# Attention stage: the k rows and the result rows are split into two 16-bit parts first and turned by transposing DMAs instead of on TensorE

## The chip, the cores and the metric

The kernel runs on one core of one Trainium2 chip. A core has five engines, each with an instruction queue that it works off in order: TensorE (PE; its weight loads are listed apart as PEld), VectorE (DVE), ScalarE (ACT), GpSimd (POOL) and SyncE (SP), which here only issues DMAs. The metric is the device time of one execution in microseconds; lower is better. Times are medians of runs, and one further execution was profiled.

## The reference, cut to what matters

```python
def _attn_ref(q, k, v, alpha):                # B, H, S, D = 4, 8, 768, 48
    state = np.zeros((B, H, D, D)); y = np.zeros_like(q)
    for t in range(S):
        state = alpha[:, :, t, :, None] * state + np.einsum('bhd,bhe->bhde', k[:, :, t], v[:, :, t])
        y[:, :, t] = np.einsum('bhd,bhde->bhe', q[:, :, t], state)
    return y

def reference(...):
    attn_out = _attn_ref(q, k, v, alpha)
    x = attn_out.transpose(0, 2, 1, 3).reshape(B * S, H * D)     # 3072 tokens x 384
    x = _moe_ref(x, ...)       # 8 experts, all of them on all tokens, Sinkhorn weights
    return _moe2_ref(x, ...)   # 8 experts, the best two of each token
```

## The kernel before, in words

The program runs three stages one after the other: the gated linear attention, a dense mixture of experts, and a sparse one. Matrix products that need more than 16 bits are made of two 16-bit parts of each operand (a high part, and what is left over), in three products.

The change touches the attention. It works in chunks of 128 tokens: 6 chunks of each of 4 batches, 24 chunks in all, numbered i (chunk c = i // 4 of batch i % 4). A table written out by hand, `order_of`, says in which order the pieces of different chunks are recorded; in each turn i, from the fifth on, that is p1 of chunk i, the four loads of chunk i+3, p3 of chunk i-2, p2 and p2b of chunk i-1, p4 of chunk i-2 and p5 of chunk i-3:

- **p1** (VectorE): two scans over alpha (`ce`, line 420, backwards; `bh`, line 424), the scaled keys `ks` (line 422) and queries `qs` (line 425); GpSimd makes `g`, the old state times the decay of the chunk, in two instructions (line 431, chunks from the fifth on); ScalarE and VectorE split v into `vh`.
- **p2**: TensorE transposes the four 128x128 blocks of `ks` (line 444) and ScalarE and VectorE split the result into the two parts of `ktok` (lines 446, 447). TensorE multiplies `ks` and `qs` into scores (line 454), ScalarE copies them out into the buffer `AFB` (which lies in the tile `acc`, line 456, two instructions), and GpSimd masks them in place (line 457, two instructions). There is one such buffer for all chunks.
- **p2b**: ScalarE and VectorE split the masked scores into the two parts of `am` (lines 464, 465).
- **p3**: TensorE multiplies `g` with `qs` (line 473), `am` with `vh` (line 478) and, in the first 20 chunks, `ktok` with `vh` (line 485); VectorE adds the latter to the state (line 489 or 491), ScalarE copies the result `y` out (line 493).
- **p4**: TensorE transposes the three blocks of `y` (line 502), ScalarE and VectorE split them into `xh` and `xl` (lines 504, 505).
- **p5**: router products of the first mixture (lines 513, 514), put into `lg` by VectorE (line 518).

Between these pieces a loop puts matmuls of the first expert (the stream: line 212, evacuated on lines 216 and 217; line 225, evacuated on line 237), a fixed amount of them for each piece, as soon as p4 of the chunk that they need has been recorded. The order on every engine is therefore fixed when the program is built. The weights of that expert are loaded and split (lines 144, 146) during the first turns.

The names of the profile: `acc` is also `AFB`, `wt` also holds loaded q and v, `bank` is a bank of PSUM, `la` and `lk` are loaded alpha and k.

Of the kernel before, what the change touches and what calls it, by code (L numbers as in the profile page):

```python
# [46 lines left out]
def kernel(ctx, tc, q, k, v, alpha, w_gate, w1a, w2a, g2w, n2w, noise, w1b, w2b, out):  # L47
# [34 lines left out]

    xh = pp.tile([128, KC, N], F16, name="xh")
    xl = pp.tile([128, KC, N], F16, name="xl")
    acc = pp.tile([128, NT, DM], F32, name="acc")
# [281 lines left out]


    INV = ap_.tile([128, NP, C2], F32, name="inv")
    nc.vector.memset(INV, 0.0)  # L370
    nc.vector.memset(INV[:, :, C2 - 1:], 1.0)

# [40 lines left out]
    def p1(i):  # L413
        c, b = order[i]
        qt, kt, at = LQ[i % NL], LK[i % NL], LA[i % NL]
        ce = CE[i % 2]
        bh = ar.tile([128, NP, C2], F32, name="bh", bufs=1)
        qs = ar.tile([128, NP, C], F32, name="qs", bufs=3)
        ks = ar.tile([128, NP, C], F32, name="ks")
        nc.vector.tensor_tensor_scan(flat(ce)[:, ::-1], flat(at)[:, ::-1], flat(INV)[:, ::-1], initial=0.0,  # L420
                                     op0=OP.mult, op1=OP.add)
        nc.vector.tensor_mul(ks, kt, ce[:, :, 2:])
        nc.vector.reciprocal(INV[:, :, 0], ce[:, :, 1])
        nc.vector.tensor_tensor_scan(flat(bh), flat(at), flat(INV), initial=0.0, op0=OP.mult, op1=OP.add)
        nc.vector.tensor_mul(qs, qt, bh[:, :, 1:C + 1])
        G = None
        if c:
            g = GB[i % 3]
            for s in range(2):
                h = slice(64 * s, 64 * s + 64)  # L430
                nc.gpsimd.tensor_mul(g[h, :, s, :], ST[b][h, :, s * D:(s + 1) * D],
                                     ce[h, :, 1:2].to_broadcast([64, NP, D]))
            G = g.rearrange("p r a d -> p r (a d)")
        vh = ar.tile([128, 2, H, D], F16, name="vh", bufs=3)
        vt = LV[i % NV]
        nc.scalar.activation(vh[:, 0], vt, AF.Copy, scale=SK)
        nc.vector.scalar_tensor_tensor(vh[:, 1], vt, SK, vh[:, 0], op0=OP.mult, op1=OP.subtract)
        R[i] = [qs, ks, G, vh]

    def p2(i):  # L440
        qs, ks, G, vh = R[i]
        pt = bank([128, NP, C])
        for r in range(NP):
            nc.tensor.transpose(pt[:, r, :], ks[:, r, :], ident)
        kt = ar.tile([128, 2, NP, C], F16, name="ktok")
        nc.scalar.activation(kt[:, 0], pt, AF.Copy, scale=SK)
        nc.vector.scalar_tensor_tensor(kt[:, 1], pt, SK, kt[:, 0], op0=OP.mult, op1=OP.subtract)
        pA = [bank([128, NP, C]), bank([128, NP, C])]
# [6 lines left out]
        for s in range(2):  # L455
            nc.scalar.activation(af[:, s], pA[s], AF.Copy, scale=SK)
            nc.gpsimd.affine_select(af[:, s], af[:, s], pattern=[[0, NP], [1, 128]], compare_op=OP.is_ge, fill=0.0,
                                    base=0, channel_multiplier=-1)
        R[i] += [kt, am]

# [6 lines left out]
    def p3(i):  # L467
# [13 lines left out]
        if c + 1 < NC:  # L481
# [6 lines left out]
            if c:  # L488
                nc.vector.tensor_add(ST[b], pv, G)
            else:  # L490
                nc.vector.tensor_copy(ST[b], pv)
        y = ar.tile([128, DM], F32, name="y")
        nc.scalar.activation(y, py.rearrange("p r a d -> p (r a d)"), AF.Copy, scale=SX / (SK * SK))
        R[i].append(y)

    def p4(i):
        c, b = order[i]
        T = c * B + b
        y = R[i][-1]
        px = bank([128, KC, 128])  # L500
        for kc in range(KC):
            nc.tensor.transpose(px[:, kc, :], y[:, kc * 128:(kc + 1) * 128], ident)
        s = slice(T * 128, (T + 1) * 128)
        nc.scalar.activation(xh[:, :, s], px, AF.Copy)
        nc.vector.tensor_sub(xl[:, :, s], px, xh[:, :, s])

# [802 lines left out]
```

## Time and profile before

| | us |
|---|---|
| median of 3 runs (lowest, highest) | 2095.74 (2094.11, 2097.69) |
| the profiled execution | 2102.97 |
| its span, first to last instruction | 2101.2 |
| what lies around the span | 1.8 |
| TensorE busy | 2016.1 (96%) |
| VectorE busy | 1229.3 (59%) |
| ScalarE busy | 725.8 (35%) |
| GpSimd busy | 625.4 (30%) |

The shares are means over stages with different limits. The attention with its part of the stream takes up about the first 247 of the 2101 us; what follows is recorded without any use of the lines above. Within the attention the unit to read is one turn, the time from one line's instruction for chunk i to the same line's for chunk i+1.

### The profile page before, as it was taken

The numbers are of one execution on the slowest core, as the hardware profiler recorded it, in microseconds if no ns is written. First come the engines' busy times: TensorE is split into PE (matmuls) and PEld (weight loads), VectorE is DVE, ScalarE is ACT, GpSimd is POOL, SyncE is SP. The second block draws the span as 40 slices with busy tenths as digits, with TensorE's granted clock in tenths as the row PEclk, the third lists the DMA queues.
The fourth block names the chain that finished last, engine by engine and source line by source line (L and its number), as shares of the span: only waits on it lengthen the run. The fifth ranks groups of instructions, "written<-read, shape, count | busy, mean of one in ns | idle before, by whom it ended". The sixth has DMA issues, their size and how long they took to land. (4 is left out here: it accounts for less than half of the span.)

```text
span 2101.2 us, 38370 instructions
## 1 busy us (share of the span) xinstructions
PE 2016.1 (96%) x16123; PEld 1361.2 (65%) x16123; DVE 1229.3 (59%) x2513; ACT 725.8 (35%) x1277; POOL 625.4 (30%) x452
## 2 busy tenths in 40 slices
PE   6999999999999999999999999999999999999996
PEld 5887656667766766677667766775556565555553
DVE  8889574765675585566557556554345655444431
ACT  5554422432342243333333333223334233333230
POOL 2433212522442253234324332230001243323322
PEclk9999999999999999999999999999999999999998
DMA  6333010100010020010001001004112334433331
GB/s 212 96 105 105 21 41 21 47 16 1 26 36 1 1 61 2 1 34 29 1 11 51 1 1 41 1 2 152 57 42 84 84 91 121 96 73 87 84 76 23
DMA packets 61855, 106.94 MB, mean 51 GB/s; under 512 B 10980, under 2 KB 44029, under 8 KB 61680
## 3 DMA queue, kind: packets, MB, share of 16 engines
q1 hardware_dynamic: 50256, 85.05, 12.7%
q0 software_dynamic: 11136, 18.89, 5.2%
q8 instruction: 127, 2.08, 0.4%
q10 hardware_dynamic: 288, 0.52, 0.1%
q14 instruction: 48, 0.39, 0.1%
HBM read 85.17 MB, written 21.63 MB: 51 GB/s over the span
## 5 line engine op out<-in xcount | busy, mean ns | idle before, releaser
L272 PE MATMUL bank<-xh,wt 128*128 128x512 f16 x1728 | 521.9, 380 | 6.2 <-DVE ss L295 3.8
L306 PE MATMUL long<-wt,hid 128*128 128x192 f16 x6048 | 508.8, 246 | 14.1 <-DVE acc L316 9.2
L291 POOL TENSOR_TENSOR hid<-ss,hid 128x1024 f16<-128x1024 f32 x144 | 307.1, 2132 | 706.1 <-ACT hid L290 651.7
L306 PEld LDWEIGHTS <-hid 128*128 128x128 f16 x6048 | 499.6, 98 | 27.0 <-issue 11.1
L272 PEld LDWEIGHTS <-wt 128*128 128x128 f16 x2592 | 253.1, 98 | 306.2 <-PE bank L272 6.1
L225 PE MATMUL bank<-wt,hid 128*128 128x384 f16 (+1 forms) x2496 | 430.5, 328 | 1.8 <-DVE hid L866 1.8
L225 PEld LDWEIGHTS <-hid 128*128 128x128 f16 (+1 forms) x2496 | 242.2, 99 | 156.6 <-issue 5.2
L272 PE MATMUL bank<-xl,wt 128*128 128x512 f16 x864 | 328.2, 380 | 0.0
L316 DVE SCALAR_TENSOR_TENSOR acc<-long,Pm,acc 128x192 f32<-128x192 f32 (+1 forms) x360 | 187.3, 533 | 169.8 <-PE long L306 167.5
L295 DVE SCALAR_TENSOR_TENSOR ss<-bank,ss 128x256 f32<-128x256 f32 x576 | 241.5, 421 | 58.3 <-ACT hid L284 39.6
L295 DVE SCALAR_TENSOR_TENSOR hid<-bank,hid 128x256 f16<-128x256 f32 (+1 forms) x288 | 158.9, 552 | 180.9 <-ACT ss L279 180.9
L290 ACT ACTIVATE hid<-ss 128x1024 f16<-128x1024 f32 x144 | 152.2, 1057 | 241.2 <-DVE ss L295 241.2
L146 DVE SCALAR_TENSOR_TENSOR wt<-wst,wt 128x1024 f16<-128x1024 f32 (+3 forms) x129 | 167.2, 1308 | 36.9 <-ACT wt L144 36.1
L278 ACT ACTIVATE hid<-bank 128x256 f16<-128x256 f32 x144 | 53.4, 371 | 382.4 <-PE bank L272 382.4
L875 POOL DMA_INDIRECT out_dram<-acc,ix x56 | 91.5, 1634 | 296.5 <-DVE acc L874 245.6
L862 PEld LDWEIGHTS <-wt 128*128 128x128 f16 x1152 | 110.9, 98 | 86.4 <-issue 4.7
L866 DVE SCALAR_TENSOR_TENSOR hid<-bank,hid 128x384 f16<-128x384 f32 (+1 forms) x128 | 74.9, 589 | 109.5 <-ACT hid L865 109.3
L865 ACT ACTIVATE hid<-bank 128x384 f16<-128x384 f32 (+1 forms) x128 | 65.8, 517 | 205.1 <-PE bank L862 201.6
L144 ACT ACTIVATE wt<-wst 128x1024 f16<-128x1024 f32 (+3 forms) x129 | 111.4, 883 | 70.9 <-DMA wst<-in_moe_w_dram 47.3
L194 PE MATMUL bank<-xh,wt 128*128 128x512 f16 x384 | 120.0, 379 | 0.7 <-DVE acc L316 0.7
L862 PE MATMUL bank<-xh,wt 128*128 128x384 f16 (+1 forms) x576 | 109.1, 343 | 0.9 <-ACT xh L852 0.9
L284 ACT ACTIVATE hid<-bank 128x512 f16<-128x512 f32 x144 | 86.0, 597 | 66.4 <-PE bank L272 66.4
(188 smaller groups left out, 1792.7 us busy)
## 6 DMA issues: line engine op xcount, KB each, us to landing
wst<-in_moe_w_dram SPq DMA_DIRECT2D x45, 512.0 KB, 3.3
wst<-in_moe_w_dram SPq DMA_DIRECT2D x60, 384.0 KB, 3.2
la<-in_alpha_dram SPq DMA_DIRECT2D x24, 260.0 KB, 2.7
lk<-in_k_dram SPq DMA_DIRECT2D x24, 256.0 KB, 3.0
wt<-in_q_dram SPq DMA_DIRECT2D x22, 256.0 KB, 3.9
out_dram<-zero SPq DMA_DIRECT2D x6, 768.0 KB, 4.4
xd<-x SPq DMA_DIRECT2D x24, 192.0 KB, 1.9
wt<-in_v_dram SPq DMA_DIRECT2D x16, 192.0 KB, 4.1
```

The source lines that it names most:

```text
L144: nc.scalar.activation(t[:, o:o + n], src, AF.Copy, scale=SW)
L146: nc.vector.scalar_tensor_tensor(t[:, o + o1:o + o1 + n], src, SW, t[:, o:o + n], op0=OP.mult, op1=OP.subtract)
L194: nc.tensor.matmul(p, w1s(e, a, kc, f), x[:, kc, s], start=(n == 0), stop=(n == 3 * KC - 1))
L225: nc.tensor.matmul(p, h(a, f, s), w2s(x, b, f), start=(f + n == 0), stop=(f == FC - 1 and n == 2))
L272: nc.tensor.matmul(p, w1s(e, a, kc, f), x[:, kc, tok], start=(n == 0), stop=(n == 3 * KC - 1))
L290: nc.scalar.activation(lefts(e, nb, j, 0, S1, 4), sums, AF.Copy)
L291: nc.gpsimd.tensor_sub(lefts(e, nb, j, 1, S1, 4), sums, lefts(e, nb, j, 0, S1, 4))
L295: nc.vector.scalar_tensor_tensor(out, p, 0.0, x, op0=OP.max, op1=op)
L306: nc.tensor.matmul(out, left(e, nb, j, a, aop)[:, q * 128:(q + 1) * 128], w2t(e, b, wop, j), start=start and n == 0, stop=stop and n == 3 ...
L316: nc.vector.scalar_tensor_tensor(a, p, Pm[:, T, e:e + 1], a, op0=OP.mult, op1=OP.add)
L862: nc.tensor.matmul(p, w1s(x, a, kc, f), xt[:, b * KC + kc, :], start=(i == 0), stop=(i == 3 * KC - 1))
L875: nc.gpsimd.indirect_dma_start(out=out, out_offset=bass.IndirectOffsetOnAxis(ap=ix, axis=0), in_=y, in_offset=None, bounds_check=N - 1, oo ...
```

## The change

Before, `ks` and `y` (32-bit) are transposed on TensorE and split into two 16-bit parts behind that. After, they are split first and a transposing DMA turns both parts in one go.

- `ks` is scaled by 256 through the start values of the scan, so that it needs no factor in the split. In p1, for the first 20 chunks, ScalarE makes the high part `kf[:, 0]`, GpSimd the low part `kf[:, 1]`, and SP issues a DMA transpose of both (8 blocks of 128x128) into `ktok`.
- p2 loses its four transposes and both instructions of the split.
- In p3 ScalarE and VectorE split `y` on its way out of PSUM, the state's sum becomes one instruction with a factor on `g`.
- In p4 only a DMA transpose of the two parts of `y` (6 blocks of 128x128) into `x2` is left; `xh` and `xl` are the two halves of `x2`.

```diff
-    xh = pp.tile([128, KC, N], F16, name="xh")
-    xl = pp.tile([128, KC, N], F16, name="xl")
+    x2 = pp.tile([128, 2 * KC, N], F16, name="x2")
+    xh, xl = x2[:, :KC], x2[:, KC:]
...
-    nc.vector.memset(INV[:, :, C2 - 1:], 1.0)
+    nc.vector.memset(INV[:, :, C2 - 1:], SK)
...
         ks = ar.tile([128, NP, C], F32, name="ks")
+        kf = ar.tile([128, 2, NP, C], F16, name="kf")
+        kt_ = ar.tile([128, 2, NP, C], F16, name="ktok")
...
         nc.vector.tensor_mul(qs, qt, bh[:, :, 1:C + 1])
+        if c + 1 < NC:
+            nc.scalar.activation(kf[:, 0], ks, AF.Copy)
+            nc.gpsimd.tensor_sub(kf[:, 1], ks, kf[:, 0])
+            nc.sync.dma_start_transpose(out=kt_.rearrange("p a r c -> p (a r) c"),
+                                        in_=kf.rearrange("p a r c -> p (a r c)"))
         G = None
...
-        R[i] = [qs, ks, G, vh]
+        R[i] = [qs, ks, G, vh, kt_]
...
-        qs, ks, G, vh = R[i]
-        pt = bank([128, NP, C])
-        for r in range(NP):
-            nc.tensor.transpose(pt[:, r, :], ks[:, r, :], ident)
-        kt = ar.tile([128, 2, NP, C], F16, name="ktok")
-        nc.scalar.activation(kt[:, 0], pt, AF.Copy, scale=SK)
-        nc.vector.scalar_tensor_tensor(kt[:, 1], pt, SK, kt[:, 0], op0=OP.mult, op1=OP.subtract)
+        qs, ks, G, vh, kt = R[i]
...
-                nc.vector.tensor_add(ST[b], pv, G)
+                nc.vector.scalar_tensor_tensor(ST[b], G, 1.0 / SK, pv, op0=OP.mult, op1=OP.add)
...
-        y = ar.tile([128, DM], F32, name="y")
-        nc.scalar.activation(y, py.rearrange("p r a d -> p (r a d)"), AF.Copy, scale=SX / (SK * SK))
+        y = ar.tile([128, 2, DM], F16, name="y")
+        py = py.rearrange("p r a d -> p (r a d)")
+        nc.scalar.activation(y[:, 0], py, AF.Copy, scale=SX / (SK * SK))
+        nc.vector.scalar_tensor_tensor(y[:, 1], py, SX / (SK * SK), y[:, 0], op0=OP.mult, op1=OP.subtract)
...
-        px = bank([128, KC, 128])
-        for kc in range(KC):
-            nc.tensor.transpose(px[:, kc, :], y[:, kc * 128:(kc + 1) * 128], ident)
         s = slice(T * 128, (T + 1) * 128)
-        nc.scalar.activation(xh[:, :, s], px, AF.Copy)
-        nc.vector.tensor_sub(xl[:, :, s], px, xh[:, :, s])
+        nc.sync.dma_start_transpose(out=x2[:, :, s], in_=y.rearrange("p a d -> p (a d)"))
```

The order on the engines moves at three places. First GpSimd, in the middle of the attention: two turns of before,

```order
L431 TENSOR_TENSOR g_112<-acc,ce_118 64x4x48 x2
L457 AFFINE_SELECT acc<-acc 128x512 x2
L431 TENSOR_TENSOR g_113<-acc,ce_119 64x4x48 x2
L457 AFFINE_SELECT acc<-acc 128x512 x2
L431 TENSOR_TENSOR g_114<-acc,ce_118 64x4x48 x2
```

and two turns of after, where the masking is line 459 and the product with the state line 439:

```order
L431 TENSOR_TENSOR kf<-ks,kf 128x512
L439 TENSOR_TENSOR g_113<-acc,ce_117 64x4x48 x2
L459 AFFINE_SELECT acc<-acc 128x512 x2
L431 TENSOR_TENSOR kf<-ks,kf 128x512
L439 TENSOR_TENSOR g_111<-acc,ce_118 64x4x48 x2
```

The subtraction for chunk i now stands ahead of the two products of chunk i, and so ahead of the masking of chunk i-1. Second ScalarE, one turn of before, from the split of v of chunk i to the split of the scores of chunk i-1,

```order
L436 ACTIVATE vh<-wt_72 128x384
L493 ACTIVATE y<-bank 128x384
L446 ACTIVATE ktok<-bank 128x512
L456 ACTIVATE acc<-bank 128x512 x2
L464 ACTIVATE am<-acc 128x1024
```

and the same turn of after, with the next one's beginning:

```order
L430 ACTIVATE kf<-ks 128x512
L444 ACTIVATE vh<-wt_71 128x384
L496 ACTIVATE y<-bank 128x384
L458 ACTIVATE acc<-bank 128x512 x2
L466 ACTIVATE am<-acc 128x1024
L517 ACTIVATE pr<-bank 128x8
```

The high part of k is now made at the head of the turn, ahead of v, y and the scores, and `xh` (line 504 of before) is gone. Third SP, one turn of after:

```order
L505 DMA_TRANSPOSE x_66<-y 128x6x128
L432 DMA_TRANSPOSE ktok<-kf 128x8x128
L366 DMA la_82<-in_alpha_dram 128x520
L366 DMA lk_79<-in_k_dram 128x512
L366 DMA wt_71<-in_q_dram 128x512
L366 DMA wt_71<-in_v_dram 128x384
```

Before, only the four loads stood there. On VectorE the split of `ktok` (line 447) and `xl` (line 505) are gone and the low part of `y` (line 497 of after) stands right behind the state's sum; the rest stands as it did.

## Rows read from the trace of the kernel before

**Rows 1.** Busy time of each engine in two stretches of the attention (windows).

```profile
core 0: us, PE busy (x) PEld busy (x) DVE busy (x) ACT busy (x) POOL busy (x), PEclk, DMA share, GB/s
43.39:199.32 155.93, 148.05 (x1873) 124.70 (x1871) 139.59 (x214) 78.56 (x156) 60.89 (x65) 1.00 0.32 103
199.32:247.50 48.18, 45.42 (x519) 36.53 (x517) 36.41 (x56) 23.71 (x47) 16.35 (x18) 1.00 0.07 22
```

**Rows 2.** Timeline of GpSimd: start, length, line, idle before and its releaser.

```profile
43.39 2.35 POOL L431 TENSOR_TENSOR g<-acc,ce 64x192 f32<-64x192 f32 x2 [7.54 <-DVE ce L420]
...
97.80 1.22 POOL L457 TENSOR_SCALAR_AFFINE_SELECT acc<-acc 128x512 f32<-128x512 f32 x2 [2.70 <-ACT acc L456]
103.21 2.35 POOL L431 TENSOR_TENSOR g<-acc,ce 64x192 f32<-64x192 f32 x2 [4.18 <-PE bank L444]
105.64 1.88 POOL L457 TENSOR_SCALAR_AFFINE_SELECT acc<-acc 128x512 f32<-128x512 f32 x2
...
199.32 2.35 POOL L431 TENSOR_TENSOR g<-acc,ce 64x192 f32<-64x192 f32 x2 [4.60 <-DVE ce L420]
```

**Rows 3.** Timeline of VectorE, from one split of scores to the next.

```profile
100.14 1.23 DVE L465 TENSOR_TENSOR am<-acc,am 128x1024 f16<-128x1024 f32 x1 [2.50 <-ACT am L464]
101.29 0.55 DVE L505 TENSOR_TENSOR xl<-bank,xh 128x384 f16<-128x384 f32 x1
101.75 0.15 DVE L518 TENSOR_TENSOR lg<-bank,pr 128x8 f32<-128x8 f32 x1
101.83 1.23 DVE L420 TENSOR_TENSOR_SCAN ce<-la,inv 128x520 f32<-128x520 f32 x1
103.09 0.69 DVE L422 TENSOR_TENSOR ks<-lk,ce 128x512 f32<-128x512 f32 x1
...
109.20 1.21 DVE L465 TENSOR_TENSOR am<-acc,am 128x1024 f16<-128x1024 f32 x1
```

**Rows 4.** Timeline of ScalarE in the same turn.

```profile
107.55 1.06 ACT L464 ACTIVATE am<-acc 128x1024 f16<-128x1024 f32 x1 [0.63 <-POOL acc L457]
```

**Rows 5.** Groups by line and shape, 43.39 to 199.32 us: busy, mean ns, idle before.

```profile
L217 DVE SCALAR_TENSOR_TENSOR hid<-bank,hid 128x512 f16<-128x512 f32 x18 | 12.2, 677 | 0.1
L447 DVE SCALAR_TENSOR_TENSOR ktok<-bank,ktok 128x512 f16<-128x512 f32 x16 | 10.8, 674 | 0.0
L444 PE MATMUL bank<-ident,ks 128*128 128x128 f32 x64 | 9.8, 275 | 0.0
L446 ACT ACTIVATE ktok<-bank 128x512 f16<-128x512 f32 x16 | 9.5, 596 | 16.6 <-PE bank L444 16.4
L502 PE MATMUL bank<-ident,y 128*128 128x128 f32 x48 | 8.1, 278 | 0.0
```

**Rows 6.** The nearest subtraction on GpSimd, whole run (groups by line).

```profile
L291 POOL TENSOR_TENSOR hid<-ss,hid 128x1024 f16<-128x1024 f32 x144 | 307.1, 2132 | 706.1 <-ACT hid L290 651.7
```

**Rows 7.** Who waited for whom, 43.39 to 199.32 us: total, times, longest.

```profile
PE bank L478 <- DVE am L465: 7.8, 12, 1.3
```

**Rows 8.** DMA, 43.39 to 199.32 us: queue (packets, MB, share); issues (KB, us to landing).

```profile
q1 hardware_dynamic: 9216, 15.80, 31.6%
...
lk<-in_k_dram SPq DMA_DIRECT2D x16, 256.0 KB, 3.0
```

**Rows 9.** Timeline of TensorE in the first two turns with stream matmuls.

```profile
21.20 0.55 PE L502 MATMUL bank<-ident,y 128*128 128x128 f32 x3
...
25.10 0.26 PE L212 MATMUL bank<-xl,wt 128*128 128x128 f16 x1 [2.06 <-DVE xl L505]
...
34.87 0.50 PE L502 MATMUL bank<-ident,y 128*128 128x128 f32 x3
...
37.61 0.22 PE L212 MATMUL bank<-xl,wt 128*128 128x128 f16 x1 [0.92 <-DVE xl L505]
```

**Rows 10.** Timeline of TensorE behind a long wait, in the next stage.

```profile
313.35 0.38 PE L272 MATMUL bank<-xh,wt 128*128 128x512 f16 x1 [2.45 <-DVE acc L235]
...
313.78 0.59 PE L272 MATMUL bank<-xh,wt 128*128 128x512 f16 x2
...
316.79 1.06 PE L272 MATMUL bank<-xh,wt 128*128 128x512 f16 x2
```

More of the change, by code (lines that the diff above doesn't have):

```diff
@@ L458, in p2 @@
                                     base=0, channel_multiplier=-1)
-        R[i] += [kt, am]
+        R[i] += [am]
     def p2b(i):
```

## Prediction, made before the changed kernel was run

> **What bounds the kernel now.** I read the windows first, to see which engine is full in the stretch that the change touches. From the product with the state of chunk 4 to that of chunk 20 [rows 2], sixteen turns, 155.93 us pass, 9.75 us a turn. In it TensorE is busy for 148.05 us and VectorE for 139.59 us [rows 1]: 9.25 and 8.72 us a turn, so TensorE idles 0.5 us a turn and VectorE 1.0. Neither has room to spare, and neither is simply full: nearly all of TensorE's idle time, 7.8 of 7.9 us, is spent before line 478 waiting for VectorE's split of the scores [rows 7]. So I took the timelines next, to see what that split waits for. It is the end of a row of steps that hand over between engines: VectorE makes `ce` and `ks`, GpSimd multiplies the state with `ce` and then masks the scores, ScalarE splits off their high part, VectorE the low part [rows 2 to 4]. In the turn shown GpSimd's products start at 103.21, right behind `ce`, the masking ends at 107.52, ScalarE is through at 108.61, and VectorE, which had other work until then, takes up the split at 109.20. So this row of steps is now some 0.6 us shorter than VectorE's own work beside it. GpSimd itself is 39% busy (60.89 of 155.93 us), with its order fixed.
>
> **The change part by part.** *Removed.* TensorE loses four and three transposes a turn, 9.8 and 8.1 us over sixteen turns, 1.12 us a turn [rows 5]; 8.13 us of its 9.25 are left. VectorE loses line 447, 0.67 us a turn [rows 5]; the low part of `y` has the shape and source of `xl` (0.55 us [rows 3]) and replaces it one for one, and the state's sum stays one instruction. VectorE is left with 8.05 us. ScalarE swaps one copy of 512 columns for another and loses `xh`. If these two engines alone set the pace, a turn would take some 0.7 to 1.1 us less.
>
> *Moved.* The work that takes their place stands elsewhere, and this decides. The subtraction of `kf` is on GpSimd ahead of the products with the state and of the masking, and it has to wait for ScalarE's `kf`, which waits for `ks` of the same turn. Before, GpSimd began its products when `ce` was there; now it begins two engines later. This closes a ring: VectorE does not reach `ks` of the next turn until it has made the split of the scores of this one, and that split now hangs on this turn's `ks`. From the end of `ks` once round:
>
> - ScalarE's `kf`: 0.60 (line 446, 512 columns [rows 5]) and 0.03 to hand over (107.52 to 107.55 [rows 2, 4]);
> - GpSimd's subtraction: half of a line 291, which does the same on 1024 columns in 2132 ns [rows 6]: 1.07, and 0.03;
> - the two products: 2.43, from 103.21 to the start of the masking at 105.64 [rows 2];
> - the two maskings to ScalarE's start: 1.91, 105.64 to 107.55 [rows 2, 4];
> - ScalarE's split of the scores: 1.06 [rows 4]; VectorE's: 0.03 and 1.15 (100.14 to 101.29 [rows 3]);
> - `lg` 0.08, `ce` 1.26, `ks` 0.69 (101.75 to 103.78 [rows 3]).
>
> That is 10.34 us. In 5 of the 16 turns line 217 stands between the split and `lg` in VectorE's order, 0.68 us each [rows 5], 0.21 on the mean: 10.55 us a turn. VectorE's own work between the end of `ks` and the split, 5.4 us now (103.78 to 109.20) and 5.3 after (0.67 less, 0.55 more), no longer covers the 7.2 us that the other engines take. So a turn gets 0.80 us longer where it could have got shorter: 16 x 0.80 = 12.8 us. The bounds: the two maskings take 1.88 us when they follow directly on the products and 1.22 when GpSimd stood waiting before them [rows 2]; with 1.22 the ring is 9.9 and the sum +2. If the products, which now follow directly on the subtraction, cost those 0.66 us more too, it is 11.2 and +23. I take the middle value, because in the ring the maskings always follow directly on the products.
>
> What else stands behind the new waits: on ScalarE, `kf` is ahead of v, of `y`, of the stream's `hid` and of the copies of the scores. All of these slip behind `ks`, but they need only be done when GpSimd is through with the products, 3.5 us after `kf`, and add up to about 3 us; this I cost at nothing, and it is the next thing to be late if GpSimd is faster than I think.
>
> *Added on SP.* A transposing DMA of k waits for GpSimd's subtraction and, for its buffer, for line 485 two turns back; behind it in SP's queue stand the four loads for a chunk three turns ahead. A load lands in 3.0 us [rows 8] and has some 29 us, so that wait is covered. k itself is needed two turns later (21 us), `y` in the router's products most of a turn later. The DMA queue is busy 31.6% of the stretch, 3.1 us a turn for 964 KB [rows 8]; the transposes add 256 and 192 KB. The trace shows no transposing DMA. By their bytes they would take 1.4 us of the 16 engines a turn; if every 256-byte row of a block costs as much as a mean packet of now (31.6% of 155.93 us x 16 / 9216 = 0.085 us), 1792 of them take 9.6 us. They differ from a load mainly in the way they write, not in bytes, so I take a value near the first, covered by the ring's slack up to some 7 us a turn.
>
> *The start and the end.* Stream matmuls of the first two turns need the first `x` at once: from line 502 to the first use of `xl` 3.9 and 2.7 us pass now [rows 9], mostly in VectorE's queue. A DMA that lands in 3.0 us or more, issued behind five loads, replaces this, though its source is ready earlier: I take +2.5 us for both turns, from -1 to +8. In the last four turns nothing of k is left; there TensorE is busy 45.42 of 48.18 us [rows 1] and loses 4 x 1.12 us, but the last `x` comes by DMA and costs about 1.5 of that back: -3, from -4.5 to 0.
>
> *Sum.* 12.8 + 2.5 - 3 = +12.3 us on the profiled execution's 2102.97 (0.34% above the median of the runs): on the median, 2095.74 + 12.3 = **2108 us**. After the attention the order is unchanged, TensorE runs nearly without a break, and nothing can take a delay up.
>
> **The rivals.** *The ring is shorter than VectorE's work* (faster): if the four steps off VectorE take 5.3 us and not 7.2, for instance because GpSimd's recorded spans overlap more than they say, VectorE sets the pace and 24 turns gain its 0.67 us, 16 us: 2080; with TensorE's 1.12 it would be 2069. For it: spans on GpSimd are rough. Against: the pair of products is 2.35 us long at each of the three places shown, and at 105.64 the masking starts only when it has ended [rows 2].
>
> *The transposes fill the DMA engines* (slower, another cause): it decides from 7.4 us a turn on for both. At 9.6 us a turn takes 12.7 with the loads, 20 turns with k cost 59 us: 2155. For it: no DMA in the trace scatters its elements over 128 rows. Against: 31.6% is little now. The Trainium skill, VectorE: DVE Perf Modes (The three transpose paths), lists 1309 ns for one 128x128 block by DMA; if the 14 blocks of a turn ran one by one at that, 18.3 us, the time would be about 2330, an estimate. Another page of the Trainium skill, DMA: Bandwidth & Descriptors (Latency and other measured facts), gives 261 GB/s for a transposing DMA with a non-contiguous middle dimension; by that both take 1.8 us, an estimate, and this rival falls away. No run shown here decides between the two.
>
> *TensorE loses its clock.* It will idle 2.4 us a turn (10.55 less 8.13), in one piece before line 478. After a wait of 2.45 us a pair of matmuls took 0.59 us at first and then 1.06 [rows 10], that is the lower of the clock's two levels, 1.2 GHz, for some 3 us, at a loss of 1.6 us. Mostly that falls into the idle time; in the 7 turns where stream matmuls stand between p3 and the next p2 it can hold up the scores: up to 11 us more, 2119.
>
> *Nothing to be measured*: the ring at its lower bound, +2, and start and end cancel: 2096.
>
> **How the numbers follow.** The ring as summed 0.43, with the lower clock 0.10, the faster case 0.18, DMA-bound 0.17, nothing 0.12. The ring's own range, from the bounds above, is 2092 (2, -1, -4.5) to 2138 (23, +8, 0, +11). To hold 8 in 10 the range reaches into both other cases: 2086 to 2155. A change under 0.2% (4.2 us) can't be told from none here. Faster 0.19 (that rival and a remainder of the ring's lower end), same 0.14, slower 0.67.
>
> **What would show it.** Right: the products with the state start 10 us or more apart from chunk 4 to 19 and directly behind the subtraction of `kf`; GpSimd waits for ScalarE's `kf`, ScalarE for VectorE's `ks`, VectorE before the split of the scores for ScalarE; TensorE's wait at `am` grows from 7.8 to some 35 us; the DMA share stays under 0.6. Wrong: turns under 9.4 us with VectorE busy throughout (the ring is shorter than thought), TensorE waiting for `ktok` or `x2` and DMA engines full (the transposes), or a gap mainly before 43 us (the start).

## The result, and the profile after

The changed kernel takes 2122.98 us (median of 4 runs, 2118.05 to 2124.61), the kernel before beside it 2096.51: a ratio of 1.0117 [1.0095, 1.0138], that is 24.5 us by the ratio and 26.5 by the medians, where +12.3 was forecast. The sign and the range hold; the size does not, and two terms of the sum missed, in opposite directions. The execution profiled of after is the fastest of its runs (2118.05 us, span 2116.3), so some 5 us of the difference of the medians don't show in it.

The windows of after, the start and then a stretch as long as that of [rows 1]:

```profile
core 0: us, PE busy (x) PEld busy (x) DVE busy (x) ACT busy (x) POOL busy (x), PEclk, DMA share, GB/s
0.00:53.40 53.40, 20.05 (x250) 18.99 (x251) 36.86 (x51) 20.53 (x34) 12.64 (x19) 0.81 0.73 216
53.40:209.00 155.60, 135.54 (x1724) 111.40 (x1722) 137.98 (x193) 68.66 (x138) 69.44 (x78) 0.98 0.63 142
```

TensorE did lose its transposes (148.05 to 135.54 us busy), VectorE hardly became freer (139.59 to 137.98), and the share of the DMA engines doubled from 0.32 to 0.63. Where the time went is read best at one instruction that each chunk has once, VectorE's scan `ce` at line 423 (420 before): chunks 3, 4, 19, 20 and 23 in after's timeline,

```profile
29.71 1.23 DVE L423 TENSOR_TENSOR_SCAN ce<-la,inv 128x520 f32<-128x520 f32 x1
53.38 1.23 DVE L423 TENSOR_TENSOR_SCAN ce<-la,inv 128x520 f32<-128x520 f32 x1
...
203.10 1.23 DVE L423 TENSOR_TENSOR_SCAN ce<-la,inv 128x520 f32<-128x520 f32 x1
214.19 1.23 DVE L423 TENSOR_TENSOR_SCAN ce<-la,inv 128x520 f32<-128x520 f32 x1
...
241.64 1.23 DVE L423 TENSOR_TENSOR_SCAN ce<-la,inv 128x520 f32<-128x520 f32 x1
```

and the same five in the kernel before, profiled once more (label before_again, span 2095.4 us):

```profile
27.09 1.23 DVE L420 TENSOR_TENSOR_SCAN ce<-la,inv 128x520 f32<-128x520 f32 x1
39.92 1.23 DVE L420 TENSOR_TENSOR_SCAN ce<-la,inv 128x520 f32<-128x520 f32 x1
...
186.19 1.22 DVE L420 TENSOR_TENSOR_SCAN ce<-la,inv 128x520 f32<-128x520 f32 x1
195.09 1.22 DVE L420 TENSOR_TENSOR_SCAN ce<-la,inv 128x520 f32<-128x520 f32 x1
...
224.19 1.23 DVE L420 TENSOR_TENSOR_SCAN ce<-la,inv 128x520 f32<-128x520 f32 x1
```

Chunk 4 is 13.5 us late (11.4 against the first profile of before, where it starts at 42.00). The fifteen turns to chunk 19 take 149.72 us for 146.27, 9.98 us a turn for 9.75: 3.5 us more. The next turn takes 11.09 for 8.90: 2.2 more. The last three take 27.45 for 29.10: 1.65 less. So in this execution the start weighs more than all turns together, and the prediction had it the other way round. Behind chunk 23 the spans differ by another 3.5 us, but 3.0 of these lie behind the first instruction of line 272, in stages that the change doesn't touch (1787.85 us against 1784.86; in the first profile of before it is 1787.85 too). The two profiles of before differ at the start by TensorE's granted clock, 0.89 in the first 40 us of the first and 1.00 in those of before_again. A term of 2 or 3 us in one profile is therefore no more than a hint.

**The start.** TensorE's timeline has two long waits in it (line 212, the stream's first matmuls with x [rows 9]):

```profile
33.61 4.00 PE L212 MATMUL bank<-x,wt 128*128 128x128 f16 x36 [11.15 <-DMA x<-y]
...
48.40 2.10 PE L212 MATMUL bank<-x,wt 128*128 128x128 f16 x18 [5.82 <-DMA x<-y]
```

Before, the first uses of the complete x (with `xl`) stood at 25.10 and 37.61 [rows 9]: x is 8.5 us later for the first chunk, 10.8 for the second. VectorE's timeline says when the low part of the first y is made:

```profile
25.45 0.54 DVE L497 SCALAR_TENSOR_TENSOR y<-bank,y 128x384 f16<-128x384 f32 x1
```

It ends at 25.99, 0.9 us after x was already in use before. That it is so late is the work of k's split. In y_only, the run below that leaves k on TensorE, the same instruction stands 3.3 us earlier, at 22.14, and y's DMA goes out as soon as it has ended; VectorE's and SyncE's timelines there:

```profile
22.14 0.55 DVE L496 SCALAR_TENSOR_TENSOR y<-bank,y 128x384 f16<-128x384 f32 x1
```

```profile
22.71 1.34 SPq L504 DMA_TRANSPOSE x<-y  x1
```

The 3.3 us are the ring at work in the first turns already. In after GpSimd's subtraction for chunk 1 (12.80 to 14.37) stands ahead of the masks of chunk 0, which start at 14.33 instead of 11.43 in y_only; the scans of chunk 2 follow 2.5 us later (18.58 for 16.04), and `qs` of that chunk takes 1.46 us instead of 0.69. The rest is SyncE's queue in after (columns: start of the issue, its length):

```profile
22.94 1.24 SPq L432 DMA_TRANSPOSE ktok<-kf  x1
24.23 0.57 SPq L115 DMA_DIRECT2D acc<-in_moe_w_dram  x1
24.89 0.43 SPq L366 DMA_DIRECT2D la<-in_alpha_dram  x1
...
26.80 0.42 SPq L115 DMA_DIRECT2D acc<-in_moe_w_dram  x1
27.31 1.22 SPq L505 DMA_TRANSPOSE x<-y  x1
...
39.44 1.24 SPq L432 DMA_TRANSPOSE ktok<-kf  x1
40.77 0.53 SPq L366 DMA_DIRECT2D la<-in_alpha_dram  x1
...
43.30 1.60 SPq L505 DMA_TRANSPOSE x<-y  x1
```

y's DMA goes out at 27.31, 1.3 us after its source is ready, behind k's transposing DMA, four loads and two pieces of weights, and x is used 6.3 us later: 0.9 + 1.3 + 6.3 = 8.5. In y_only x is used 4.3 us after the issue, at 27.03, and at 38.35 for the second chunk. For the second y the DMA ahead of it is that of chunk 3's k (39.44). It waits for its buffer, which line 487 of chunk 1 reads until 39.4, and that line itself stands on TensorE behind the matmuls that had waited for the first x; so the first wait feeds the second. Four loads and a weight stand behind the DMA, and y, ready at 40.44, goes out at 43.30. During the first wait the granted clock falls to 0.50, the lower level of 1.2 GHz (26 to 38 us), and the 36 matmuls behind it take 4.00 us. This is not what sets after apart: in g_first, below, the same 36 take 4.00 us with a granted clock of 1.00 in the rows, and chunk 4 starts only 0.7 us earlier.

**The turns.** The ring of the prediction is there. GpSimd's timeline of one turn [rows 2], and the waits of the sixteen turns (us in total, times, longest):

```profile
95.41 1.57 POOL L431 TENSOR_TENSOR kf<-ks,kf 128x512 f16<-128x512 f32 x1 [5.23 <-ACT kf L430]
96.94 1.75 POOL L439 TENSOR_TENSOR g<-acc,ce 64x192 f32<-64x192 f32 x2
98.76 1.22 POOL L459 TENSOR_SCALAR_AFFINE_SELECT acc<-acc 128x512 f32<-128x512 f32 x2
```

```profile
POOL kf L431 <- ACT kf L430: 78.8, 15, 5.6
ACT kf L430 <- DVE ks L425: 50.8, 16, 3.4
...
DVE am L467 <- ACT am L466: 14.2, 13, 2.1
...
PE bank L480 <- DVE am L467: 12.6, 14, 1.0
...
PE bank L212 <- DMA x<-y: 3.1, 3, 1.2
```

GpSimd waits for ScalarE's `kf`, ScalarE for `ks`, VectorE for the split of the scores, as forecast. But GpSimd's three steps take 1.53 + 1.82 + about 1.22 = 4.57 us and not 5.44, and TensorE's wait is 12.6 us [rows 7: 7.8], not some 35.

### The profile page after: what moved, and what is told of

It is laid out like the page before. It is cut to its first block, busy times and chain, and to the rows that moved or that the text cites. A ratio compares the mean times of both kernels' runs of the same rounds, so it can differ in the third digit from the quotient of the medians.

```text
span 2116.3 us, 38169 instructions
## 1 busy us (share of the span) xinstructions
PE 2000.0 (95%) x15955; PEld 1345.0 (64%) x15955; DVE 1228.4 (58%) x2489; ACT 710.6 (34%) x1249; POOL 639.9 (30%) x472
## 5 line engine op out<-in xcount | busy, mean ns | idle before, releaser
L272 PE MATMUL bank<-x,wt 128*128 128x512 f16 x2592 | 568.0, 380 | 6.3 <-DVE ss L295 3.8
L862 PE MATMUL bank<-x,wt 128*128 128x448 f16 (+1 forms) x1152 | 215.2, 340 | 0.9 <-ACT x L852 0.9
L194 PE MATMUL bank<-x,wt 128*128 128x512 f16 x576 | 130.1, 379 | 0.7 <-DVE acc L316 0.7
L874 DVE TENSOR_SCALAR acc<-bank,wc 128x384 f32<-128x384 f32 (+1 forms) x56 | 34.5, 616 | 117.8 <-PE bank L225 117.8
```

The source lines that it names most:

```text
L194: nc.tensor.matmul(p, w1s(e, a, kc, f), x[:, kc, s], start=(n == 0), stop=(n == 3 * KC - 1))
L272: nc.tensor.matmul(p, w1s(e, a, kc, f), x[:, kc, tok], start=(n == 0), stop=(n == 3 * KC - 1))
L862: nc.tensor.matmul(p, w1s(x, a, kc, f), xt[:, b * KC + kc, :], start=(i == 0), stop=(i == 3 * KC - 1))
```

## The experiments

All times are medians; ratios are against the kernel before on the same chip in the same minutes (2096.5 us beside after, 2098 to 2100 beside the others). The two right columns come from each profile: the start of `ce` of chunk 4, and the mean turn from chunk 4 to 19.

| label | us | ratio, 95% | ce of chunk 4 | us a turn |
|---|---|---|---|---|
| before_again (1 run) | 2097.06 | | 39.92 | 9.75 |
| after | 2122.98 | 1.0117 [1.0095, 1.0138] | 53.38 | 9.98 |
| k_only | 2114.26 | 1.0073 [1.0061, 1.0086] | 44.16 | 10.40 |
| y_only | 2101.74 | 1.0012 [1.0003, 1.0020] | 43.04 | 9.76 |
| late_split | 2104.98 | 1.0029 [1.0018, 1.0040] | 50.22 | 9.64 |
| loads_after_y | 2111.21 | 1.0064 [1.0050, 1.0077] | 46.96 | 10.06 |
| g_first | 2116.25 | 1.0094 [1.0079, 1.0110] | 52.67 | 9.99 |
| late_loads_after_y | 2107.62 | 1.0048 [1.0034, 1.0062] | 51.35 | 9.63 |
| old_start_late | 2096.46 | 0.9994 [0.9985, 1.0003] | 40.07 | 9.72 |
| old_start | 2108.32 | 1.0039 [1.0026, 1.0053] | 40.19 | 10.23 |
| y_act_queue | 2119.57 | 1.0093 [1.0077, 1.0109] | 50.42 | 10.46 |
| ktok3 | 2116.67 | 1.0079 [1.0064, 1.0094] | 49.34 | 10.35 |
| old_start_y_first | 2098.09 | 0.9996 [0.9983, 1.0008] | 42.63 | 9.73 |
| sub_on_vector | 2101.99 | 1.0010 [0.9998, 1.0022] | 39.94 | 9.76 |
| k_late | 2093.52 | 0.9972 [0.9960, 0.9984] | 41.59 | 9.48 |
| old_start_late_y_act | 2135.10 | 1.0167 [1.0152, 1.0183] | 41.55 | 12.08 |

**Each half alone.** k_only keeps y's transposes on TensorE (the diff below, against the change), y_only those of k in p2 with the copy and the split behind them; before_again is the kernel before.

> The kernel before, profiled once more. The profiles of before and after differ by 15.1 us (spans 2101.2 and 2116.3), the medians by 26.5. If the first profile of before is some 5 us long by chance, this one should be near 2095 us with the difference in one stretch; if a profile always costs some 6 us, it is near 2102 again and turn by turn the same.

> Only k is split first and turned by DMA; the result y is transposed on TensorE as before. Theory A (the loss is the wait of the first stream matmuls for the transposed x, queued on SP behind loads and k): the wait is gone, ce of chunk 4 starts near 43 us instead of 53.4, and the whole is within 6 us of before. Theory B (the loss is the ring through ScalarE and GpSimd that the split of k closes): nearly all of the loss stays, 12 us or more slower than before, turns of 10 us or more from chunk 4 to 19.

> Only y is split first and turned by DMA; k is transposed on TensorE as before. Theory A: the loss of the start stays, ce of chunk 4 starts near 51 us or later, and the whole is 8 to 20 us slower than before. Theory B: without the ring a turn costs less than before (TensorE loses 0.33 us, VectorE nothing), so the time is within 5 us of before or better.

```diff
-        nc.sync.dma_start_transpose(out=x2[:, :, s], in_=y.rearrange("p a d -> p (a d)"))
+        for kc in range(KC):
+            nc.tensor.transpose(px[:, kc, :], y[:, kc * 128:(kc + 1) * 128], ident)
+        nc.scalar.activation(xh[:, :, s], px, AF.Copy)
+        nc.vector.tensor_sub(xl[:, :, s], px, xh[:, :, s])
```

before_again comes near 2095 us, but the 5.8 us between the spans of the two profiles of before are not in one stretch: 2.1 lie at the start, 0.8 in the fifteen turns, 3.0 behind line 272. k_only has the longer turns of theory B (10.40 us; that VectorE keeps `xl`, 0.55 us [rows 3], in the ring is the likely reason for the 0.4 us above after) with the start of theory A; y_only has neither (9.76, within 5 us of before, as B said). At the start k alone costs 4.2 us and y alone 3.1, both together 13.5 (2.2, 1.0 and 11.4 against the first profile of before). In y_only the first two DMAs of y go out at 22.71 and 33.56 instead of 27.31 and 43.30. Of the 4.6 us of the first, 3.3 are the later source and 1.3 the queue. So it is k's part, by its split as much as by its DMA ahead of y's, that makes x late.

**k's split out of the ring, and the order on SyncE and GpSimd.** late_split records the split and the DMA of k behind the scores of the turn. loads_after_y moves the loads of the chunk three turns ahead behind y's DMA; late_loads_after_y does both. g_first records GpSimd's subtraction behind the products with the state. The diff shows the order of a turn in late_split (pk holds the split and the DMA) and then in loads_after_y.

> All of the change, but the split of k and its DMA are recorded behind the scores of the chunk before (behind p2 in the turn), so that GpSimd makes the products and the masking first and the ring is open. Theory B: turns from chunk 4 to 19 fall from 9.98 to about 9.2 us, 12 us or more are gained on the changed kernel. Theory A: the start stays as long (ce of chunk 4 near 53 us), and the turns, which the ring lengthens by little, give at most 6 us.

> All of the change; the four loads for chunk i+3 are recorded behind p4, so that on SP the transposing DMA of y stands ahead of them and not behind. Theory A2 (the start is long because y's DMA is issued and queued behind five loads): the first stream matmuls begin 3 us earlier or more (they began at 33.6), ce of chunk 4 starts at 47 us or before instead of 53.4, and 5 to 8 us are gained on the changed kernel. Rival A3 (it is long because SP has to wait for the buffer of k and because a transposing DMA takes 3 to 5 us itself): ce of chunk 4 stays within 3 us of 53.4.

> The late split of k and the loads behind p4, together. If the losses of ring and queue add up, the start falls from the 50.2 us of the late split by as much as in the run with the loads behind p4 alone, and the time comes to 2098 to 2102 us, within 0.2% of before; if the start is set by the transposing DMAs themselves, it stays near 2105.

> All of the change; only on GpSimd the subtraction of k is recorded behind the two products with the state, so that these start with ce again while ScalarE makes the high part. Theory B (ring): the ring is 1 us or more shorter, below VectorE's own turn, and turns from chunk 4 to 19 fall from 9.98 to 9.5 us or less; 6 us or more are gained on the changed kernel and the start stays at 53 us. Rival (the turns are set by something else, such as TensorE's clock or the DMA queues, which are busy 63% now): turns stay at 9.9 or more.

```diff
-    return ("p1", 0), ("load", -3), ("p3", 2), ("p2", 1), ("p2b", 1), ("p4", 2), ("p5", 3)
+    return ("p1", 0), ("load", -3), ("p3", 2), ("p2", 1), ("pk", 0), ("p2b", 1), ("p4", 2), ("p5", 3)
-    return ("p1", 0), ("load", -3), ("p3", 2), ("p2", 1), ("p2b", 1), ("p4", 2), ("p5", 3)
+    return ("p1", 0), ("p3", 2), ("p2", 1), ("p2b", 1), ("p4", 2), ("load", -3), ("p5", 3)
```

With the split behind the scores a turn takes 9.64 us, less than before: the ring was real, and this opens it. The whole is 18 us below the change, as theory B said, though its 9.2 us a turn were not reached. Of the 16.0 us between the two profiles the fifteen turns give 5.1, the turn behind them 2.8 and the start 3.2; 4.9 lie behind chunk 23. The start stays late there (50.22), because y's DMA still stands behind k's. The low part of y is ready at 23.57 and 36.12, but SyncE's queue holds it until k's DMA is out:

```profile
25.84 1.23 SPq L449 DMA_TRANSPOSE ktok<-kf  x1
27.17 1.26 SPq L510 DMA_TRANSPOSE x<-y  x1
...
41.11 1.23 SPq L449 DMA_TRANSPOSE ktok<-kf  x1
42.43 1.27 SPq L510 DMA_TRANSPOSE x<-y  x1
```

loads_after_y shows the other side: turns of 10.06, but the start 6.4 us earlier, as theory A2 said, and the whole 0.53% (11 us) below the change, more than its 5 to 8. g_first misses its 9.5 us: its mean turn is 9.99, of which one of 12.40 us behind a wait of 2.19 us for x; the other fourteen take 9.82. Behind the products the subtraction still stands ahead of the masks, so it stays in the ring. Its whole is 0.23% better, and the turn from chunk 19 to 20 takes 9.13 us. late_loads_after_y starts no earlier than late_split (51.35), is no faster than it and misses its forecast: there, too, y's DMA goes out right behind k's (27.48 behind 26.15, 42.61 behind 41.28; y ready at 23.89 and 36.29), so the loads were not what held it.

**The start taken back.** old_start leaves the first four chunks on TensorE, with p2, p3 and p4 as in the kernel before for them, and is the change from chunk 4 on; old_start_late does the same on top of late_split; old_start_y_first also puts y's DMA ahead of k's in each turn.

> The change as it was made, but k and y of the first four chunks stay on TensorE as in the kernel before (the 32-bit y of those four costs an own tile); everything from chunk 4 on is the change. Theory (most of the loss is the start: x comes late there, 11 to 13 us at the fourth scan of VectorE): the scan of chunk 4 starts at about 40 to 42 us again, and the whole is 11 to 13 us below the change, 10 to 14 us above the kernel before, about 2110. Rival (the loss lies in the 16 turns, as the prediction had it): only 2 to 3 us come back, about 2120.

> The late split of k, and in the first four chunks both k and y are transposed on TensorE as before. Theory A: ce of chunk 4 starts within 2 us of before (39.9), the later turns are as in the late split (9.64 us), and the time is 3 to 5 us shorter than before. If the start was long for another reason (the split work on ScalarE and GpSimd, the new scan values), ce of chunk 4 stays 4 us or more late.

> The first four chunks on TensorE, the split and DMA of k in a piece of its own, which now stands behind y's transposing DMA in each turn and not ahead of it. In the run before with this start TensorE waited 3.2 us for x at 116 us and then worked at half clock, and one turn took 15.1 us instead of 9.7. Theory (this wait came from y's DMA standing behind k's): the turn takes about 10 us, and the whole is 2090 to 2094, 4 to 8 us below the kernel before (0.996 to 0.998). Rival (x is needed there just as it lands, whatever stands ahead): the long turn stays, 2096 to 2098, ratio 0.999 to 1.0.

```diff
-        if c + 1 < NC:
+        if 4 <= i < NT - B:
             nc.scalar.activation(kf[:, 0], ks, AF.Copy)
```

old_start is the run that decides: 1.0117 falls to 1.0039, that is 16 us of the 24.5 come back (give or take 5 by the two intervals; 11 to 13 were expected, 2 to 3 by the rival), and chunk 4 starts at 40.19. The scans' new start values stay in that run, so they are not the cause. The other 8 us are turns: 10.23 us, 0.48 more than before. old_start_late, without the ring as well, has the start expected but is level with before, not 3 to 5 us below it. In it one turn (chunk 12 to 13) takes 15.06 us; TensorE's timeline and the window of that turn:

```profile
119.44 4.02 PE L212 MATMUL bank<-x,wt 128*128 128x256 f16 x18 [3.24 <-DMA x<-y]
```

```profile
114.90:129.96 15.06, 10.72 (x123) 8.63 (x124) 8.68 (x15) 4.71 (x9) 4.63 (x5) 0.77 0.54 105
```

x comes 3.24 us late, and then 18 matmuls take 4.02 us where they take 2.14 at full clock (granted clock of the turn 0.77). old_start_y_first removes that wait and its long turn (9.67), as expected, and gains nothing all the same, against its expectation: the turn behind it takes 11.67 us at a granted clock of 0.85, and GpSimd's subtraction now falls beside VectorE's `ce`, which takes 1806 ns on the mean instead of 1227.

**The queue.** ktok3 gives the transposed k a third buffer, y_act_queue issues y's DMA from ScalarE, and old_start_late_y_act does that in old_start_late.

> The change, with three buffers instead of two for the transposed k, so that k's transposing DMA of a chunk no longer waits on SyncE for the state update two chunks before. Theory (in the second chunk of the start this wait holds the loads and y's transposing DMA behind it): the second wait for x falls from 5.8 us to about 3, and the whole by 2 to 3 us, to about 2120. Rival (y's issue waits for y's low part and the landing alone): no change, 2122 to 2124.

> The change, with y's transposing DMA issued from ScalarE instead of SyncE, so that it no longer stands behind k's transposing DMA and the loads. Theory 1 (the order on SyncE's queue makes x late at the start): y's issue comes right behind its low part, 1.3 us earlier for the first chunk and about 3 us for the second, the waits for x at the start fall from 20 us to about 15, and the whole falls by 3 to 6 us, to 2117 to 2120; ScalarE pays some 1.2 us a turn for the issue, which lengthens the ring only if it falls between kf and am. Theory 2 (x is late because the transposing DMA shares the engines with the loads and weights): the issue is earlier, the landing is not; the start stays at 53 us and the whole at 2122 or above.

> As the run at 0.9994 (first four chunks on TensorE, k's split behind the scores), with y's transposing DMA issued from ScalarE. Theory 1 (there y's DMA stood behind k's on SyncE's queue, x came 3.2 us late in one turn, and that turn took 15.1 us): the turn takes 9.5 to 10.5, the whole 2091 to 2094, ratio 0.996 to 0.998. Theory 2 (x is needed just as it lands, and ScalarE's 1.2 us for the issue lengthens the handover of the scores): ratio 0.999 to 1.003, TensorE waits for x at about 116 us as before or waits longer before the split of the scores.

```diff
-        kt_ = ar.tile([128, 2, NP, C], F16, name="ktok")
+        kt_ = ar.tile([128, 2, NP, C], F16, name="ktok", bufs=3)
-        nc.sync.dma_start_transpose(out=x2[:, :, s], in_=y.rearrange("p a d -> p (a d)"))
+        nc.scalar.dma_start_transpose(out=x2[:, :, s], in_=y.rearrange("p a d -> p (a d)"))
```

With the third buffer the DMA of chunk 3's k goes out at 33.73 instead of 39.44, y's at 39.59, right when its source is ready; the second wait for x is 3.07 us instead of 5.82, chunk 4 starts 4.0 us earlier, and the whole is 0.38% (8 us, give or take 5) better, more than expected. In the execution profiled 3.3 of the 4.0 us are lost again in one turn of 13.26 us (9.96 in after) with a granted clock of 0.74, so its profile shows less of the gain than its runs. From ScalarE the first y goes out at 25.89, x is used at 28.78 instead of 33.61 and the first wait is 6.31 instead of 11.15: for the first chunk SyncE's queue, and the transfers issued on it, held x for 4.8 us. But the second wait grows to 8.44, and in the turns this version loses part of it (10.46; two of them take 14.34 and 12.12 us at 0.76 and 0.86 of the clock); the whole is what theory 1 said. What it waits for is plain in old_start_late_y_act; SyncE's and ScalarE's queues,

```profile
118.03 1.24 SPq L449 DMA_TRANSPOSE ktok<-kf  x1
```

```profile
121.14 1.40 ACTq L528 DMA_TRANSPOSE x<-y  x1
122.58 0.60 ACT L216 ACTIVATE hid<-bank 128x512 f16<-128x512 f32 x1 [4.62 <-PE bank L498]
```

y's low part is ready at 117.91, but its DMA starts 3.11 us after k's on the other queue, as long as `ktok` takes to land in after (3.1 us), and ScalarE stands still for it: 12.08 us a turn, and a whole outside what either theory said (1.0167). In the program as built ScalarE's transposing DMA waits for that of k to end, and the other way round: in y_act_queue SyncE waits, by its profile, 17.1 us between 10 and 60 us for y's DMA before two of k's. The Trainium skill asks for just this (DMA: Bandwidth & Descriptors, Silent corruption: two transposing streams in flight at once): transposing DMAs of two queues must not be in flight together. The trace agrees in that those shown here were not.

**GpSimd's place, and y left on TensorE.** sub_on_vector is old_start with the subtraction for k's low part on VectorE. k_late is late_split with y on TensorE throughout, and k too in the first four chunks.

> The first four chunks on TensorE as in the run before with that start (1.0039), and the subtraction for k's low part on VectorE behind qs instead of on GpSimd. In the change GpSimd's subtraction takes 1.57 us and stands in the ring, and VectorE's qs, which runs at the same time, takes 1.47 us where it took 0.82 before. Theory 1 (GpSimd's place in the ring costs the turns their time, and the two engines slow each other down in that moment): qs is back at 0.82, the subtraction costs VectorE about 0.69, GpSimd starts its products at ce again, a turn takes 9.6 to 9.75 us instead of 10.23, and the whole is 7 to 10 us below that run: ratio 0.999 to 1.001. Theory 2 (VectorE's own work sets the turn): no gain, ratio 1.003 to 1.005.

> k of the first four chunks and y of all chunks on TensorE as in the kernel before; k from chunk 4 on split behind the scores and turned by the DMA. TensorE loses 0.6 us a turn against before, VectorE 0.67. Theory 1 (what takes the gain of the two runs at 0.9994 and 0.9996 is y's DMA: TensorE's wait for x and the half clock behind it, one turn of 15 us): no wait for x and no such turn, 9.4 to 9.6 us a turn, 2090 to 2095 beside 2098, ratio 0.996 to 0.9985. Theory 2 (the row of steps from ce over GpSimd's products to the split of the scores sets the turn as before, and work taken from TensorE and VectorE is worth nothing): 9.7 to 9.8 us a turn, ratio 0.999 to 1.001.

```diff
-            nc.gpsimd.tensor_sub(kf[:, 1], ks, kf[:, 0])
+            nc.vector.tensor_sub(kf[:, 1], ks, kf[:, 0])
```

sub_on_vector takes 9.76 us a turn for 10.23, and the whole falls from 1.0039 to 1.0010, 6 us (give or take 4), at the edge of what theory 1 said: GpSimd's place in the ring cost that. The groups of instructions (busy us, mean ns of one), in after

```profile
L428 DVE TENSOR_TENSOR qs<-wt,bh 128x512 f32<-128x512 f32 x15 | 22.0, 1465 | 0.5
L439 POOL TENSOR_TENSOR g<-acc,ce 64x192 f32<-64x192 f32 x29 | 24.4, 840 | 1.1
L431 POOL TENSOR_TENSOR kf<-ks,kf 128x512 f16<-128x512 f32 x15 | 23.5, 1566 | 86.4 <-ACT kf L430 73.7 <-issue 12.7
```

and in sub_on_vector:

```profile
L428 DVE TENSOR_TENSOR qs<-wt,bh 128x512 f32<-128x512 f32 x14 | 11.5, 823 | 0.5
L431 DVE TENSOR_TENSOR kf<-ks,kf 128x512 f16<-128x512 f32 x15 | 11.5, 766 | 0.0
```

```profile
L439 POOL TENSOR_TENSOR g<-acc,ce 64x192 f32<-64x192 f32 x30 | 34.3, 1142 | 66.5 <-PE bank L493 38.7 <-DVE ce L423 26.7
```

On GpSimd the subtraction makes VectorE's `qs` 0.64 us longer; on VectorE it would cost 0.77 itself. So the 0.67 us that VectorE lost with line 447 came back almost whole in another instruction. k_late has no DMA for y, no wait for x, the full clock in the turns, and 9.48 us a turn:

```profile
53.40:198.00 144.60, 136.55 (x1730) 114.88 (x1729) 127.15 (x191) 74.16 (x149) 77.81 (x79) 1.00 0.50 134
```

At 0.9972 [0.9960, 0.9984] it beats the kernel before and the change, as theory 1 said. Against old_start_late (0.9994), from which it differs by y alone, this says that y's DMA was worth less than y's three transposes (0.22%, give or take 0.15).

## Why the prediction was wrong in size

**The start** is the step that failed: +2.5 us, from -1 to +8, where the profiles show 11.4 to 13.5 and giving it back is worth 16 us (old_start). The prediction priced there the DMA of y as if it were alone: it "replaces" the 3.9 and 2.7 us from line 502 to the use of x, "though its source is ready earlier". For y alone that is about right. In y_only the source is ready at 22.69, 2.4 us before the first use of `xl` in the kernel before, x is used 1.9 and 0.7 us later than there [rows 9], and chunk 4 starts 1.0 to 3.1 us late. What it left out is k's part in the same turns. It counted the ring from chunk 4 on, but the ring makes y's source 3.3 us later in the first turns already (25.99). And it costed what stands ahead of y in SyncE's queue by the issues alone: k's DMA, which waits for its buffer and holds four loads and y behind it, was looked at for the loads and for k, not for y (ktok3: 8 us; loads_after_y: 11 us; these overlap and don't add up).

**The ring** was right in mechanism (late_split and sub_on_vector open it, and the turns go from 9.98 and 10.23 to 9.64 and 9.76) and too large: 10.55 us a turn and 12.8 us in sixteen turns were forecast; 9.98 are measured in after and 10.23 where the start is undisturbed, 3.5 us in fifteen turns and 16 x 0.48 = 7.7 in sixteen. The products and masks were priced by the rows 2.43 and 1.91; they took 1.82 and 1.22, while the subtraction took 1.53 and not 1.10. The reason given for 1.88 against 1.22 (masks that follow directly on the products) was wrong: in after they follow directly and take 1.22. What differs is what VectorE does at that moment (last section).

**Luck.** The two errors have opposite signs. Between the two profiles that the forecast and the result came with, 15.1 us lie, near the +12.3, but as 11.4 for 2.5 at the start, 4.9 for 12.8 in sixteen turns and -1.2 for -3 behind them.

**TensorE's clock**, a rival with up to 11 us, is real but smaller in after. The turn from chunk 19 to 20 there:

```profile
203.10:214.19 11.09, 10.45 (x90) 7.60 (x90) 8.72 (x14) 4.64 (x9) 4.43 (x5) 0.70 0.81 166
```

A granted clock of 0.70 instead of 1.00, and 11.09 us against 9.62 in the turn before: 1.5 us. In old_start three turns have 0.84 to 0.86 and take 10.83 to 12.29 us. It shows behind waits of TensorE, for the scores or for x; k_late, which has no wait for x, has no such turn from chunk 4 to 23.

**The transposes fill the DMA engines** is refuted for the turns: they put 0.31 of the engines' time, some 3 us a turn, on top of the loads, between the bounds of 1.4 and 9.6; `ktok` is waited for nowhere on TensorE, x for 3.1 us in sixteen turns. The prediction put a wait for x in the turns at nothing; it is small in after, but 3.24 us and a slow turn in old_start_late.

```profile
q1 hardware_dynamic: 36788, 21.77, 62.0%
...
ktok<-kf SPq DMA_TRANSPOSE x16, 3.1
x<-y SPq DMA_TRANSPOSE x15, 4.6
```

**The end** was forecast at -3 us and gave -1.65 over three turns; 0.5 of that is lost again up to the first instruction of line 272 (86.81 us from the last `ce` for 86.35), where TensorE awaits the last x for 1.9 us. **Faster by a shorter ring** did not come: taking the split out of GpSimd's order brings turns of 9.64, not of VectorE's 8.05 us. Why nothing could bring turns near what TensorE or VectorE have to do is not settled: in k_late GpSimd still waits 47.8 us for `ce` between 54 and 198 us, ScalarE 26.1 for the scores, so the older row of steps around the scores is the likely bound, argued and not tried. Nor was the late split run with y's DMA ahead of k's from the first chunk on, so how much of the start the order on SyncE alone could save is not known.

## What to carry to other kernels

When work moves from an engine to a DMA, ask first when its source is really ready, with the rest of the change in place, and what stands ahead of it in the issuing queue, with the waits of each of those DMAs; do this for the first turns apart, where nothing is buffered yet. Don't price the halves of a change one by one: at the start y's half alone cost 1 to 3 us and both together 11 to 13. Look for what a moved instruction stands ahead of in the new engine's order, and put work that is needed two turns later behind what is needed now. A half that pays can hide in a change that doesn't: k by DMA, split late and begun after the start, is worth 0.28% (give or take 0.12).

## What the runs showed of the hardware

- GpSimd and VectorE slow each other down in operations on f32 tensors. VectorE's `qs` takes 0.69 us where GpSimd is idle (start of before), 0.82 beside the masks or products and 1.47 beside the subtraction; `ce` 1.23 alone and 1.81 on the mean beside it; a pair of products takes 2.35 us when VectorE scans `bh` and 1.75 when it has done so; the subtraction 1.16 us on the mean in late_split and 1.57 in after. The masks take 1.88 us at 105.64 in before, beside `qs` and the split of v, and 1.22 at 98.76 in after, beside operations of VectorE that take an input from PSUM. The Trainium skill (SBUF — State Buffer, SBUF: two separate sides) has a rule for this: a VectorE operation with two inputs in SBUF and a GpSimd operation that reads SBUF lock each other out for a whole instruction. The trace agrees, as far as spans on GpSimd, which are rough, can show it. VectorE's timeline in the turn whose GpSimd rows are shown above:

```profile
94.79 1.24 DVE L427 TENSOR_TENSOR_SCAN bh<-la,inv 128x520 f32<-128x520 f32 x1
96.06 1.47 DVE L428 TENSOR_TENSOR qs<-wt,bh 128x512 f32<-128x512 f32 x1
```

  The subtraction is down from 95.41 to 96.98: `bh` runs until 96.03, so 0.95 us are left for itself, less than its half of line 291 [rows 6]. `qs` is down from 96.06 to 97.53, of which 0.55 us lie behind the subtraction's end, somewhat less than the 0.69 it takes alone. By that reading the ring holds a step that the prediction left out, VectorE's `bh` ahead of the subtraction, and the ring is cheaper in all three of GpSimd's own steps.
- A transposing DMA of 6 or 8 blocks mostly holds SyncE's queue for 1.22 to 1.24 us (1.60 in one of the rows shown), three times as long as a load (0.38 to 0.53). In the turns it lands in 3.1 us (k, 8 blocks) or 4.6 (y, 6 blocks, behind loads; 3.0 in old_start_late).
- After a wait of 3 us for x TensorE ran at about half its clock, and the turn lost 5 us and not 3 (15.06 us, against 9.67 in old_start_y_first, where the wait was gone, and 9.27 in k_late).
- Slow matmuls don't always show in the granted clock: the first 36 with x take 4.00 us in after, with 0.50 in its rows from 26 to 38 us, and 4.00 in g_first, with 1.00 there; 18 of them take 1.17 us later on.
